# Key start, mask rows by DMA and a new instruction order in a fused sparse-attention and MLP kernel

## The chip, the cores and the metric

The kernel runs on one core of a Trainium2 chip. The metric is the device time of one execution in microseconds (us), as a median over several executions. Shorter is better.

The engines are named as the profile names them. PE is the matmul engine and PEld its weight loads, DVE is the vector engine, ACT the scalar engine, POOL the general one, and SP the engine that only issues DMA. A `q` after an engine's name is its instruction queue issuing DMA.

## The reference, cut to what matters

Block-sparse attention over 32 heads (4 batches of 8), 768 tokens, 64 dimensions, followed by a residual MLP that mixes tokens and then channels:

```python
scores = (q @ k.T) / 8                     # per head, 768 x 768
mask = window | first/last block | 3 random key blocks per query block    # 24 x 24 blocks of 32
attn = softmax(where(mask, scores, -1e9))
x = attn @ v                               # heads side by side: 4 x 768 x 512
u = x + lam * (w_tok @ (alpha1 * x + beta1))
out = u + lam * (relu((alpha2 * u + beta2) @ w_ch1) @ w_ch2)
```

## The kernel before

Heads are handled in 16 pairs, each pair in nine units. A unit is a score matmul group (L1020), one exp of 128 x 1024 on ACT (L1058), a multiplication and matmuls with the values (L1082). Token mixing (L1303) and channel mixing (L1450, L1530) of one batch run beside the attention of later ones.

Queries and keys come in as rows, so they are cast to bf16 and transposed on PE before the first score matmul can run. A query operand has 88 partitions: 64 dimensions and 24 **mask rows**, which add the random blocks' mask in the same matmul. The mask rows are the same for every head. They are computed once, into the first head of operand slot 0, and three more places (the second head of slot 0, and both heads of slot 1) need a copy of 24 x 768 bf16, which is 36 KB.

The start, cut:

```python
nc.sync.dma_start(q2f[:, 0, :], pair_ap(q, 0, 0)[:, 0, :])
nc.scalar.dma_start(k2f[:, 0, :], pair_ap(k, 0, 0)[:, 0, :])       # all keys of head 0 at once
# ...
keep_warm(6, 512); keep_warm(2, P)                                 # PE work without a use
# ... mask matmuls into bq_ps ...
first_cast(0, 0, nc.vector.tensor_copy)                            # queries of head 0
nc.scalar.activation(qx2[0][MB, 0, HS:S], bq_ps[1][0:NBLK, 0:HS], AF.Copy, bias=-BIG, scale=BIG)
nc.vector.tensor_scalar(out=qx2[0][MB, 0, 0:HS], ...)              # the two halves of the mask rows
nc.scalar.copy(out=relp[:, 0, 1, 0:P], in_=k2f[:, 0, 0:P])         # keys 0..127
nc.vector.tensor_copy(out=relp[:, 0, 1, P:HS], in_=k2f[:, 0, P:HS])
keep_warm(3, P)
for w, bk, o0, o1, cp in (
    (0, gbT[0], 0, 3, nc.vector.tensor_copy),                      # w = 0 queries, 1 keys
    (1, gbT[1], 0, 1, nc.scalar.copy),
    (1, gbT[2], 1, 3, nc.vector.tensor_copy),
):
    t = transposes(bk[:], lambda o: relp[:, 0, w, ts(o, P)], range(o0, o1))
    keep_warm(1 if w else 4, P)
    for r in range(2):
        cp(out=qkr[0][:, w, 0, o0:o1, r, :], in_=t[r * D : (r + 1) * D, o0:o1])
```

Everything after that goes through a list scheduler. Each operation has dependencies and a due time, shifted by an entry of a table `DUE` of about 1,400 tuned numbers. The scheduler simulates the engines at build time, and each engine then runs its instructions in that fixed order. The row copies were three scheduled DVE operations, and from unit 4 of the first pair (the first unit with blocks of its second head) a score matmul depends on the first of them:

```python
pl = Plan(..., dict(PE=5950, ACT=6100, DVE=6300, POOL=4000, SP=4000))   # when each engine is free, ns
# ...
for j in range(1, 4):
    def e_row(op, j=j):
        nc.vector.tensor_copy(out=qx2[j // 2][MB, j % 2, :], in_=qx2[0][MB, 0, :])
    ROWS.append(pl.dve(("row", j), dve(768, 4), (2, 6, 7)[j - 1], e_row))
# ...
if pi == 0:
    deps = [] if u < 4 else deps + ROWS[:1]
```

The softmax here doesn't subtract the row's maximum and nothing guards it: scores larger than these inputs give would overflow.

## Time and profile before

| | before |
|---|---|
| time | 305.74 us, median of 3 (305.52 to 305.75) |
| span of the profiled run | 304.0 us |
| start of the first channel-mixing matmul, called T | 54.51 us |
| span minus T | 249.49 us |
| first exp | 6.61 us |

The prediction below reads the engine table, slices, chain and timeline. How to read them: a timeline line gives the start and length of a run of equal instructions, then engine, line, operation, output and inputs. In brackets stands how long the engine was idle before it and what ended that wait. `x3` at the end means three instructions back to back. The chain of waits is followed backwards from the last instruction, so its shares say through which lines the end was set.

### The profile page before, as it was taken

How to read it: one execution, taken by the hardware profiler on the slowest of the kernel's cores; microseconds unless marked ns; L12 is line 12 of the kernel's file. 1: busy time of each engine (PE TensorE's matmuls, PEld its weight loads, DVE VectorE, ACT ScalarE, POOL GpSimd, SP SyncE). 2: the span in 40 equal slices, each digit the busy share in tenths (PEclk: the TensorE clock that was granted, in tenths of full speed). 3: DMA queues.
4: the chain of work that ended last, by engine and by line, in shares of the span. 5: the costliest groups of instructions: out<-in, count | busy, mean ns of one | idle time of the engine just before them, and what ended most of it. 6: DMA issues, size and time to landing. Idle time of an engine off the chain costs nothing.

```text
span 304.0 us, 7157 instructions
## 1 busy us (share of the span) xinstructions
PE 297.9 (98%) x2977; PEld 187.1 (62%) x2998; DVE 234.1 (77%) x441; ACT 177.5 (58%) x242; POOL 44.6 (15%) x71
## 2 busy tenths in 40 slices
PE   8999999999999999999999999999999999999996
PEld 4777888666656575566655565555664674565453
DVE  7779889988998995989878886668869681997212
ACT  4999999978778755775486756554557720000000
POOL 9457441150110120010000000000000000000000
PEclk9999999999999999999999999999999999999999
DMA  7999999999885969183252332050021004000111
GB/s 154 199 264 202 205 205 178 188 201 138 156 122 99 144 117 164 41 122 79 43 119 47 108 65 56 36 133 16 37 52 49 25 0 122 37 0 0 71 66 72
DMA packets 50672, 31.38 MB, mean 103 GB/s; under 512 B 27784, under 2 KB 47056, under 8 KB 50640
## 3 DMA queue, kind: packets, MB, share of 16 engines
q0 software_dynamic: 17520, 15.47, 32.8%
q1 hardware_dynamic: 32796, 15.06, 22.2%
q8 instruction: 23, 0.38, 0.5%
q10 hardware_dynamic: 324, 0.39, 0.4%
q14 instruction: 9, 0.07, 0.1%
HBM read 30.78 MB, written 6.29 MB: 122 GB/s over the span
## 4 chain that ended last, share of the span: by engine, by line
PE 91%; DVE 6%; ACT 1%; issue 1%; ACTq 0%
PE gb L1450 27%; PE gb L1530 27%; PE gb L1082 11%; PE gb L1303 9%; PE sps L1020 5%; PE sps L1039 4%; PE gb L1039 3%; PE gb L517 2%; PE gb L485 1%; DVE qk L579 1%; DVE a1p L1265 1%; DVE a1p L1254 1%; ACT eT L1058 0%; ACT qk L577 0%; DVE x_sb L1101 0%
## 5 line engine op out<-in xcount | busy, mean ns | idle before, releaser
L1058 ACT ACTIVATE eT<-sps 128x1024 f16<-128x1024 f32 x114 | 110.7, 1029 | 8.8 <-PE gb L1082 5.7
L1450 PE MATMUL gb<-uT,w1b 128*128 128x384 bf16 (+1 forms) x512 | 91.9, 326 | 0.0
L1530 PE MATMUL gb<-w2b,hts 128*128 128x512 bf16 (+2 forms) x379 | 87.2, 370 | 1.1
L1450 PEld LDWEIGHTS <-w1b 128*128 128x128 bf16 x512 | 48.5, 98 | 33.7 <-issue 1.9
L1063 DVE TENSOR_TENSOR eT<-eT,msk 128x1024 f16<-128x1024 f16 x90 | 59.7, 685 | 6.5 <-ACT eT L1058 6.4
L1530 PEld LDWEIGHTS <-hts 128*128 128x128 bf16 x400 | 36.6, 98 | 38.9 <-issue 1.9
L1058 ACT ACTIVATE eT<-gb 128x512 f16<-128x512 f32 x60 | 32.5, 594 | 33.7 <-PE gb L1039 31.8
L1497 DVE TENSOR_SCALAR hts<-gb,b1t 128x384 bf16<-128x384 f32 x73 | 44.9, 617 | 9.1 <-PE gb L1450 7.5
L1082 PEld LDWEIGHTS <-eT 128*128 128x128 f16 x1152 | 44.3, 97 | 10.8 <-issue 2.2
L1082 PE MATMUL gb<-vext,eT 128*128 128x65 f16 x1152 | 47.9, 193 | 0.1
L1489 ACT ACTIVATE hts<-gb,b1t 128x384 bf16<-128x384 f32 x55 | 31.5, 582 | 21.3 <-PE gb L1450 19.1
L1303 PE MATMUL gb<-a1p,wtokT 128*128 128x256 bf16 (+1 forms) x360 | 37.0, 251 | 0.0
L1552 DVE TENSOR_TENSOR ot<-x_sb,gb 128x512 f32<-128x512 f32 (+2 forms) x25 | 16.6, 665 | 25.9 <-PE gb L1530 25.9
L1303 PEld LDWEIGHTS <-wtokT 128*128 128x128 bf16 x360 | 29.5, 98 | 6.9 <-issue 1.9
L1020 PE MATMUL sps<-qk 88*128 88x512 bf16 (+1 forms) x144 | 31.3, 325 | 0.5 <-ACT eT L1058 0.3
L1327 DVE TENSOR_TENSOR x_sb<-x_sb,gb 128x512 f32<-128x512 f32 (+1 forms) x26 | 16.7, 642 | 2.9 <-PE gb L1303 2.5
L1101 DVE TENSOR_TENSOR x_sb<-gb,rcp 128x384 f32<-128x384 f32 x32 | 17.8, 558 | 1.1
L1039 PE MATMUL sps<-qk 64*128 64x256 bf16 x180 | 17.9, 305 | 0.0
L1098 DVE RECIPROCAL rcp<-gb 128x6 f32<-128x6 f32 x32 | 6.2, 193 | 13.2 <-PE gb L1082 13.2
L1039 PEld LDWEIGHTS <-qk 64*128 64x128 bf16 x240 | 9.3, 94 | 11.5 <-issue 7.1
L1341 DVE TENSOR_TENSOR ub<-x_sb,a_bc 128x512 bf16<-128x512 f32 (+1 forms) x26 | 16.1, 645 | 0.3
L648 POOL DMA_DIRECT2D q<-in_q_dram x15 | 10.7, 710 | 35.3 <-DMA qk<-q 29.7
(70 smaller groups left out, 173.4 us busy)
## 6 DMA issues: line engine op xcount, KB each, us to landing
out_dram<-ot SPq DMA_DIRECT2D x23, 256.0 KB, 2.0
v<-in_v_dram POOLq DMA_DIRECT2D x16, 192.0 KB, 7.9
k<-in_k_dram POOLq DMA_DIRECT2D x15, 192.0 KB, 6.5
q<-in_q_dram POOLq DMA_DIRECT2D x15, 192.0 KB, 7.2
w1b<-in_moe_w_ch_dram POOLq DMA_DIRECT2D x4, 512.0 KB, 11.4
w2b<-in_moe_w_ch_dram POOLq DMA_DIRECT2D x4, 512.0 KB, 16.9
qk<-qk SPq DMA_DIRECT2D x20, 96.0 KB, 3.0
wtk<-in_moe_w_tok_dram POOLq DMA_DIRECT2D x3, 384.0 KB, 8.6
```

The costliest lines, as they stand in the source:

```text
L1020: nc.tensor.matmul(spsT[sl(key[0])][:, o : o + w], kx2[i][0:KC, a, ts(jt, P)], qx2[i][0:KC, a, c : c + w], start=True, stop=True,)
L1039: nc.tensor.matmul(half(key, r)[:, o : o + w], kd[i][rows, h, g, :], qx2[i][rows, h, c : c + w], start=True, stop=True,)
L1058: nc.scalar.activation(out_, in_, AF.Exp, bias=EXPB, scale=SCALE)
L1063: nc.vector.tensor_tensor(out=e, in0=e, in1=msk[:, :, x : x + 512], op=ALU.mult)
L1082: nc.tensor.matmul(bk[:, t * VW : t * VW + D + 1], eTt[sl(("eT", i))][:, ts(col, P)], vx[:, a, jt, 0 : D + 1], start=(r == 0), stop=(r >= ...
L1101: nc.vector.tensor_tensor(out=x_sb[:, s0 : s0 + NT, h * D : (h + 1) * D], in0=o[:, :, 0:D], in1=rc[:].unsqueeze(2).broadcast_to([P, NT, D] ...
L1303: nc.tensor.matmul(bank(bk)[:, j * wp * P : (j + 1) * wp * P], wtokT[:, s, ts(m * g + j, P)], a1p[sl(ak)][:, s, 0:wp, :].rearrange("p w c ...
L1327: nc.vector.tensor_tensor(out=s, in0=s, in1=tp, op=ALU.add)
L1450: nc.tensor.matmul(bank(bk)[:, 0 : HS + w0], w1b[:, dk, ts(f, P)], rhs[dk], start=(dk == 0), stop=(dk == 3),)
L1489: nc.scalar.activation(htsT[hk][:, f, :], bank(bk)[:, w0 : HS + w0], AF.Relu, bias=b1t[:, f : f + 1], scale=1.0,)
L1497: nc.vector.tensor_scalar(out=htsT[hk][:, f, :], in0=bank(bk)[:, w0 : HS + w0], scalar1=b1t[:, f : f + 1], scalar2=0.0, op0=ALU.add, op1=A ...
L1530: nc.tensor.matmul(bank(ck)[:, cs], htsT[hk][:, nk, ts(mt, P)], w2h["t"][:, nk, cs], start=(nk == 0), stop=(nk == 15),)
```

## The change

Four things are done at once:

1. The first 128 key columns are loaded, cast and transposed ahead of the rest, to start the first score matmul earlier. The other 256 key columns are cast (`kr`), transposed (`kt`) and copied (`kc`) by scheduled operations.
2. The three row copies leave DVE and become DMA transfers issued on SP.
3. The transposes and copies are in another order and on other engines, and the warm-up matmuls between them are put behind them.
4. The due table is tuned anew for this start, which moves instructions of the whole kernel.

```diff
-    nc.scalar.dma_start(k2f[:, 0, :], pair_ap(k, 0, 0)[:, 0, :])
+    for c in (slice(0, P), slice(P, HS)):
+        nc.scalar.dma_start(k2f[:, 0, c], pair_ap(k, 0, 0)[:, 0, c])
 ...
+    nc.scalar.copy(out=relp[:, 0, 1, 0:P], in_=k2f[:, 0, 0:P])
     first_cast(0, 0, nc.vector.tensor_copy)
 ...
-    nc.scalar.copy(out=relp[:, 0, 1, 0:P], in_=k2f[:, 0, 0:P])
-    nc.vector.tensor_copy(out=relp[:, 0, 1, P:HS], in_=k2f[:, 0, P:HS])
-    keep_warm(3, P)
+    for j in range(1, 4):
+        nc.sync.dma_start(qx2[j // 2][MB, j % 2, :], qx2[0][MB, 0, :])
     for w, bk, o0, o1, cp in (
-        (0, gbT[0], 0, 3, nc.vector.tensor_copy),
         (1, gbT[1], 0, 1, nc.scalar.copy),
-        (1, gbT[2], 1, 3, nc.vector.tensor_copy),
+        (0, gbT[0], 0, 2, nc.vector.tensor_copy),
+        (0, gbT[2], 2, 3, nc.scalar.copy),
     ):
 ...
-        keep_warm(1 if w else 4, P)
 ...
-    keep_warm(3, P)
+    keep_warm(8, P)
-        dict(PE=5950, ACT=6100, DVE=6300, POOL=4000, SP=4000),
+        dict(PE=5600, ACT=5800, DVE=5600, POOL=4000, SP=4000),
 ...            (three DVE row operations out; kr, kt and two kc in)
+    ROWS = [landed(("row", j), 8200) for j in range(3)]
 ...
-            deps = [] if u < 4 else deps + ROWS[:1]
+            deps = [] if u < 1 else KREST[:1] if u == 1 else KREST if u < 4 else deps + ROWS[:1]
 ...            (the table DUE: all its numbers replaced)
```

`landed(..., 8200)` tells the scheduler to take the rows as being there at 8.2 us. The real wait is a semaphore.

## The prediction

> **What bounds the kernel now.** I read the page's engine table and slices first, to see which engine is full and when.
>
> ```profile
> PE 297.9 (98%) x2977; PEld 187.1 (62%) x2998; DVE 234.1 (77%) x441; ACT 177.5 (58%) x242; POOL 44.6 (15%) x71
> ...
> PE   8999999999999999999999999999999999999996
> ...
> DVE  7779889988998995989878886668869681997212
> ACT  4999999978778755775486756554557720000000
> ```
>
> PE (TensorE) looks full everywhere, but matmul ends are modelled, so I take PE's rate from the chain instead. ACT (ScalarE) is full only in slices 2 to 8, from about 8 to 61 us; DVE (VectorE) is at eight or nine tenths there. So there are two stages: a front of about 55 us, in which the exps on ACT release everything, and a long rest. The chain of work that ended last, asked for the stretch from 57 us to the end, then for 9 to 57 us, confirms it:
>
> ```profile
> by line: PE gb L1450 33.8%; PE gb L1530 33.4%; PE gb L1082 10.4%; PE gb L1303 9.8%; PE sps L1039 5.3%; PE gb L1039 3.9%; PE sps L1020 1.2%; issue 0.5%; DVE ot L1552 0.3%; PE gb L485 0.2%; PE gb L807 0.2%
> ...
> by line: PE sps L1020 26.2%; PE gb L1082 17.1%; PE gb L517 10.0%; PE gb L1303 8.7%; DVE qk L579 7.3%; issue 4.2%; DVE a1p L1265 3.8%; DVE a1p L1254 3.6%; ACT eT L1058 2.9%; ACT qk L577 2.8%; DVE x_sb L1101 2.4%; DVE wtokT L579 2.3%; DVE x_s
> ```
>
> After 57 us, all but about 1% of the chain is PE streaming: no start-up change can shorten that, only move it. Before 57 us the chain changes hands between PE, DVE and ACT. The hinge is the first channel-mixing matmul (L1450, 512 of them, 27% of the chain): from then on PE has a store of work. I call its start T. It is in the timeline, with the start-up that decides when exps begin:
>
> ```profile
> 4.49 0.48 ACT L530 ACTIVATE qk<-gb 24x384 bf16<-24x384 f32 x1 [0.95 <-PE gb L522]
> ...
> 4.99 0.30 ACT L541 CAST relp<-k2f 128x128 bf16<-128x128 f32 x1
> ...
> 5.61 0.55 ACT L553 COPY qk<-gb 64x128 bf16<-64x128 bf16 x2 [0.32 <-PE gb L517]
> ...
> 6.61 2.85 ACT L1058 ACTIVATE eT<-sps 128x1024 f16<-128x1024 f32 x3 [0.45 <-PE sps L1020]
> ...
> 6.67 0.77 DVE L997 COPY qk<-qk 24x768 bf16<-24x768 bf16 x2
> ...
> 8.80 0.51 PE L517 MATMUL gb<-identb,relp 128*128 128x128 bf16 x6 [0.52 <-DVE relp L512]
> ...
> 9.84 12.68 ACT L1058 ACTIVATE eT<-sps 128x1024 f16<-128x1024 f32 x13 [0.37 <-PE sps L1020]
> ...
> 53.36 0.36 DVE L579 COPY uT<-gb 128x384 bf16<-128x384 bf16 x1
> ...
> 54.51 0.82 PE L1450 MATMUL gb<-uT,w1b 128*128 128x385 bf16 x4
> ```
>
> The reader should see three things. The mask activation (L530) and the key cast stand in line on ACT before the first exp. The row copies L997 (0.77 us here, 0.35 more at 7.73) delay DVE's casts, PE then waits 0.52 us for those, and ACT 0.37 us for PE. And T is 54.5 us, just after DVE's last copy into uT.
>
> **What the Trainium skill says.** "VectorE: DVE Perf Modes", in its perf-mode tier table, lets a bf16 SBUF copy run four times faster than one element a cycle; 768 elements in 0.35 us (the single L997 copy) agrees, and shows that little DVE time is there to save. "DMA: Bandwidth & Descriptors", section on the anatomy of one DMA, gives a transfer about 2 us of fixed cost, most of it completion; small SBUF copies in this trace (qk<-qk, 96 KB) land in a median 3.0 us, so longer. "ScalarE: Activation LUTs", section on what ACT_TABLE_LOAD costs, measured about 1283 ns; here it is 1.28 us, from 2.26 us. "TensorE: Matmul & The Clock Gate", section on the back-to-back gap, has columns/2.4 + 2.5 ns warm, 216 ns for 512; four L1530 matmuls take 0.86 us of the chain, 215 ns each, in agreement.
>
> **The start, step by step.** Splitting the key load adds one issue on ACT's queue (0.36 us, as L452), so the table load moves from 2.26 to about 2.63 and ends at about 3.9. The cast of the first 128 key columns (0.30) then fits in ACT's former idle time before L530, ending near 4.2, against 5.29. It is off the path. The mask matmuls are not touched: L530's inputs come at 4.45, so it still ends at 4.97. The transposes of the first keys (PE) are done before that, where formerly they ended after 5.34. ACT now does two key copies (0.27 each, to 5.53) and, new, two copies of the third query slot (about 6.08). The first score matmul needs the first two query slots (two 64x256 DVE copies of 0.29 from 4.75) and the first keys, so starts near 5.4 instead of 5.98. But the first exp needs the third query slot as well: copies end at 6.08, two matmuls of 256 columns and their latency follow, exp at about 6.5. **The first exp gains only about 0.1 us**, although the first matmul gains 0.6. This is where I differ from the plan's own starting numbers, which have ACT free 0.3 us earlier.
>
> DVE loses the three row copies (0.77 + 0.35 = 1.1 us). The other key columns still need one 0.55 cast and two 0.29 copies, only later. The four casts and copies end by about 7.5, then the two casts of the second head (0.36 each) by 8.2, and the six transposes need no wait past the fourth exp's release. So **the 0.37 us hole before the fourth exp closes**. Exps after the first few are about 0.4 to 0.5 us earlier.
>
> **The rest of the front, from the new order.** I listed both kernels' instructions in order and multiplied counts by durations of the profile.
>
> ACT: exps cost 0.953 us each (7.61 for 8). Ahead of the 45th exp the kernel before has three 64x768 copies (0.75 each, as they pass in the timeline); the changed one has five such copies. That costs 1.5 us more than the start gained. The 43rd exp, which lets the 45th score block go, would end at 6.5 + 43 x 0.953 + 5 x 0.75 + about 1 us of leftover idle = 52.2.
>
> DVE: from the first query copy (5.22) to the last first-half uT copy (53.72 at its end) I count 45.2 us of work in 48.5. In the new order the same stretch holds 42.5 us, because the row copies left and two copies moved to ACT, with small shifts of other work. With the same 3.3 us of idle, starting at 4.75, it would end at 50.5.
>
> So ACT rather than DVE sets the new T. In the changed order the first L1450-type matmul comes directly after that 45th score block, so T is about 52.2 plus 0.45 for the three score matmuls, **52.7 (51.7 to 54) instead of 54.5: 1.8 us**.
>
> But the work left behind differs. Weighting each matmul with columns/2.4 (30.5 ns for the 65-column ones, from 24 in 0.73 us), PE has 44.6 us of useful work ahead of T before, and 43.4 after: 28 attention matmuls and some transposes are put off. That work comes back later: 1.2 x 1.04 = 1.25 us (1.04 from 245.7 us elapsed after T over 234.6 of such work). **Net: 1.8 - 1.25 = 0.55 us.**
>
> After T, the new order puts more work between exps: 16.8 us between the 45th and 54th score blocks instead of 10.6. There are few PE holes to fill: from T to the last score matmuls of this stage, at 65.6, PE had 11.1 us for 10.6 of work. I add 0.2 us. For the 200 us after that I add 0.3 us for a re-tuned order: by my column count its overhead there is about 10 us, mostly fixed per matmul, and in the chain only 1.2 us is "issue". Four warm-up matmuls fewer are worth nothing, they fill idle time.
>
> Sum: 0.55 + 0.2 + 0.3 = about 1.1 us. **Predicted: 304.6 us**, from 305.74.
>
> **Rivals.**
> 1. *The DMA for mask rows becomes the wait.* Three 24x768 copies are issued on SP after 5.0 and would land between 7.5 and 8.5 by the 3.0 us above. The fifth score block needs the first near 9.9. For it: the DMA line is at nine tenths through the front, and loads on POOL take 6.5 to 8 us. PE works in order, so a row landing at 11 would cost the exps 1 us: 305.5. Against: the same hardware queue's q2f copies, five times larger, land in 3.2 us. I give it 15%.
> 2. *ACT is the real bound and gets worse.* Five copies instead of three, and after the 45th exp a run of uT copy, three copies and two relus (about 3.8 us) with no exp between. If PE's attention matmuls starve there, T's gain is given back: 306 to 306.5. For it: ACT at nine tenths. Against: L1450 work is then ready, and it needs no exps.
> 3. *DVE was the real bound.* The chain passes through DVE from 17 to 33 us. If freeing 2.7 us of DVE moves T by the whole 3.2 us (53.7 to 50.5), the net gain is 2 to 2.5 us: 303.2. Against: ACT has no matching slack.
> 4. *The new order decides after T.* It may close holes that my counts don't see, or open some; PE lost about 4 us between 6 and 57 us by counts and a few more later. I give it 1 us either way.
>
> **Range and chances.** Rivals 1, 2 and 4 together give the upper end, 306.3; rivals 3 and 4 the lower, 302.7. Two per cent is 6.1 us. All the PE time lost in the front after 6 us is about 4 us, so a gain that large would need the later stage too: chance 0.03. A loss that large needs a stall that nothing here shows: 0.02. Within 2%: 0.95.
>
> **What would show it right or wrong.** Right: the first exp at about 6.5 while the first score matmul starts near 5.4; no ACT idle before the fourth exp; the first channel-mixing matmul at 51.7 to 54; rows landed before 9 us with no PE wait on them; PE's useful counts unchanged. Wrong: a PE wait on the DMA rows; the first exp near 6.3 (then ACT's copies are cheaper than I say); T after 54.5, or T near 50.5 (DVE was the bound); or T as predicted and the total not, which puts the cause in the order after T.

## More of the kernel before

One more view shows what the DMA engines did at the start. The rows of the windows view give: the stretch, its length, busy time of PE, PEld, DVE, ACT and POOL (with instruction counts), the granted PE clock, the busy share of the DMA engines, and GB/s.

```profile
6.00:9.00 3.00, 2.21 (x19) 1.31 (x20) 2.90 (x12) 2.55 (x4) 2.37 (x5) 1.00 1.19 152
9.00:20.00 11.00, 10.94 (x165) 8.67 (x163) 8.25 (x19) 10.34 (x12) 4.91 (x8) 1.00 1.17 224
```

From 6 us on the DMA share is at or above 1: the engines are full with bulk loads of the next heads and of the weights.

## The result, and the profile after

The changed kernel took **307.64 us** (median of 6, 307.09 to 307.82) against 305.75 us for the kernel before in the same rounds (median of 6, 305.52 to 306.29). The ratio is 1.0058, 95% interval 1.0045 to 1.0071. All ratios here are the mean time of one kernel's fast runs over that of the other's in the same rounds, so they are not quite the ratios of the medians. The time lies 1.3 us above the predicted range, and the sign is wrong.

The engine table and the PE, DVE and ACT slices of the changed kernel, with its chain over the whole span below them:

```profile
PE 300.1 (98%) x2994; PEld 187.4 (61%) x2994; DVE 230.4 (75%) x435; ACT 179.9 (59%) x247; POOL 45.0 (15%) x71
...
PE   8899999999999999999999999999999999999995
...
DVE  5398997998967789977789986758879871997122
ACT  4799999896668765789767755754566510000000
...
PE 95%; DMA 2%; ACT 1%; SPq 0%; issue 0%; DVE 0%; ACTq 0%
```

DVE lost 3.7 us of work (234.1 to 230.4), as intended, and its second slice (7.6 to 15.3 us) fell from 7 to 3 tenths. The chain has a new entry: 2% of it is now DMA. Before, there was none. The chain from 9 to 57 us says which transfer that is, first as shares and then as one piece with start and length:

```profile
by line: PE sps L1051 35.1%; PE gb L1113 22.7%; PE gb L1334 16.8%; DMA qk<-qk 11.3%; PE gb L521 11.0%; ACT eT L1089 4.6%; issue 1.7%; PE gb L1481 1.4%; PE gb L489 0.1%; ACTq L1089 0.0%
...
6.70 5.41 DMA qk<-qk
```

`qk<-qk` of 36 KB are the mask rows. The chain counts from the wrong issue here: 6.70 is the third copy's, and a partial update of that copy at 12.11 is the last one before PE goes on. The score matmul needs the first copy, and PE waits on that copy's semaphore. By the semaphore updates in the trace, the three copies were issued at 4.99, 5.92 and 6.70 and complete at 12.05, 12.88 and 13.23. So **the copy that PE waited for took 7.05 us from issue to landing**, and the 5.41 us and 11.3% above are too small. DVE, which had at least 19% of this stretch before (7.3, 3.8, 3.6, 2.4 and 2.3), is gone from it. The lines of the timeline that answer to those shown of before (L1051 scores, L1089 exps, L1481 first channel-mixing matmul):

```profile
4.39 0.89 PE L521 MATMUL gb<-identb,relp 128*128 128x128 bf16 x4
...
4.99 2.56 SPq L547 DMA_DIRECT2D qk<-qk  x3
...
5.93 1.06 PE L1051 MATMUL sps<-qk 88*128 88x512 bf16 x3
...
7.02 1.02 ACT L1089 ACTIVATE eT<-sps 128x1024 f16<-128x1024 f32 x1 [0.94 <-PE sps L1051]
...
8.71 2.85 ACT L1089 ACTIVATE eT<-sps 128x1024 f16<-128x1024 f32 x3 [0.66 <-PE sps L1051]
...
12.18 0.38 PE L1051 MATMUL sps<-qk 88*128 88x512 bf16 x1 [1.10 <-DMA qk<-qk]
...
12.59 1.02 ACT L1089 ACTIVATE eT<-sps 128x1024 f16<-128x1024 f32 x1 [1.03 <-PE sps L1051]
...
55.04 0.82 PE L1481 MATMUL gb<-uT,w1b 128*128 128x385 bf16 x4
```

Read it from above. The first exp starts at 7.02 us, not at 6.61. There is a hole of 0.66 us before the second exp. The fifth unit's score matmul (the first of the second head, so the first that needs a copied mask row) waits 1.10 us for the DMA, and ACT waits 1.03 us behind it. T is 55.04, not 54.51 and far from the predicted 52.7.

A second thing shows when each span is cut at T. The **span is T plus a remainder that belongs to the order of instructions**:

| kernel | order | span | T | span − T | median us | ratio (95%) |
|---|---|---|---|---|---|---|
| before | old | 304.0 | 54.51 | 249.49 | 305.75 | |
| changed | new | 305.8 | 55.04 | 250.76 | 307.64 | 1.0058 (1.0045 to 1.0071) |
| a_dve_rows | new | 304.1 | 53.68 | 250.42 | 305.88 | 1.0000 (0.9981 to 1.0019) |
| a_warm | new | 307.3 | 56.58 | 250.72 | 308.88 | 1.0096 (1.0076 to 1.0116) |
| a_dve_warm | new | 304.0 | 53.57 | 250.43 | 305.84 | 1.0015 (0.9973 to 1.0056) |
| b_dma_rows | old | 305.8 | 56.06 | 249.74 | 308.24 | 1.0076 (1.0043 to 1.0109) |
| a_dve_late | new | 304.6 | 54.18 | 250.42 | 306.31 | 1.0024 (1.0005 to 1.0042) |
| a_dve_late_warm | new | 305.1 | 54.69 | 250.41 | 306.00 | 1.0001 (0.9984 to 1.0017) |
| a_hold | new | 305.8 | 55.04 | 250.76 | 307.49 | 1.0058 (1.0043 to 1.0073) |
| a_old_start | new | 303.8 | 53.34 | 250.46 | 305.67 | 1.0006 (0.9986 to 1.0025) |
| a_best | new | 304.3 | 53.88 | 250.42 | 305.96 | 1.0001 (0.9986 to 1.0015) |
| b_late | old | 303.3 | 53.85 | 249.45 | 305.47 | 0.9996 (0.9983 to 1.0010) |
| after_2 (changed again) | new | 305.5 | 54.75 | 250.75 | 307.28, one run | |
| before_2 (before again) | old | 303.8 | 54.34 | 249.46 | 305.55, one run | |

Over all fourteen traces the remainder is 249.45 to 249.74 with the old order and 250.41 to 250.76 with the new one, while T varies by more than 3 us. So whatever a start-up edit is worth is read off T, and the new order costs about 1 us after T whatever the start is. The two last rows are single executions, whose state is unknown; they serve for their timelines only. Spans are rounded to 0.1 us, and the remainders with them. In the rounds of the experiments the kernel before had medians of 305.76 us (for all up to a_old_start) and 305.65 us (for a_best and b_late). All experiments gave correct results.

### The profile page after: what moved, and what is told of

It is laid out like the page before. It is cut to its first block, busy times and chain, and to the rows that moved or that the text cites. A ratio compares the mean times of both kernels' runs of the same rounds, so it can differ in the third digit from the quotient of the medians.

```text
span 305.8 us, 7180 instructions
## 1 busy us (share of the span) xinstructions
PE 300.1 (98%) x2994; PEld 187.4 (61%) x2994; DVE 230.4 (75%) x435; ACT 179.9 (59%) x247; POOL 45.0 (15%) x71
## 3 DMA queue, kind: packets, MB, share of 16 engines
q0 software_dynamic: 17520, 15.47, 32.4%
## 4 chain that ended last, share of the span: by engine, by line
PE 95%; DMA 2%; ACT 1%; SPq 0%; issue 0%; DVE 0%; ACTq 0%
PE gb L1481 27%; PE gb L1561 27%; PE gb L1113 12%; PE gb L1334 11%; PE sps L1051 7%; PE sps L1070 4%; PE gb L1070 3%; PE gb L521 2%; DMA qk<-qk 2%; PE gb L489 1%; ACT eT L1089 1%; SPq L547 0%; DVE ot L1583 0%; ACT qk L535 0%; PE gb L810 0%
## 5 line engine op out<-in xcount | busy, mean ns | idle before, releaser
L1089 ACT ACTIVATE eT<-sps 128x1024 f16<-128x1024 f32 x114 | 110.9, 1031 | 5.9 <-PE sps L1051 4.4
L1481 PE MATMUL gb<-uT,w1b 128*128 128x384 bf16 (+1 forms) x512 | 90.9, 326 | 0.0
L1561 PE MATMUL gb<-w2b,hts 128*128 128x512 bf16 (+2 forms) x400 | 89.3, 370 | 0.0
L1481 PEld LDWEIGHTS <-w1b 128*128 128x128 bf16 x512 | 48.7, 98 | 33.8 <-issue 1.9
L1089 ACT ACTIVATE eT<-gb 128x512 f16<-128x512 f32 x60 | 32.5, 594 | 40.0 <-PE gb L1070 39.9
L1528 DVE TENSOR_SCALAR hts<-gb,b1t 128x384 bf16<-128x384 f32 x72 | 44.1, 617 | 11.2 <-PE gb L1481 9.4
L1113 PEld LDWEIGHTS <-eT 128*128 128x128 f16 x1152 | 43.5, 97 | 10.7 <-issue 3.5
L1520 ACT ACTIVATE hts<-gb,b1t 128x384 bf16<-128x384 f32 x56 | 32.3, 583 | 20.8 <-PE gb L1481 13.2
L1051 PE MATMUL sps<-qk 88*128 88x512 bf16 (+1 forms) x144 | 32.6, 333 | 1.7 <-DMA qk<-qk 1.1
L1051 PEld LDWEIGHTS <-qk 88*128 88x128 bf16 x144 | 12.4, 99 | 7.5 <-issue 3.1
L651 POOL DMA_DIRECT2D q<-in_q_dram x15 | 10.6, 707 | 40.5 <-DMA qk<-q 35.0
```

What stands on the lines that cost most here:

```text
L1051: nc.tensor.matmul(spsT[sl(key[0])][:, o : o + w], kx2[i][0:KC, a, ts(jt, P)], qx2[i][0:KC, a, c : c + w], start=True, stop=True,)
L1089: nc.scalar.activation(out_, in_, AF.Exp, bias=EXPB, scale=SCALE)
L1113: nc.tensor.matmul(bk[:, t * VW : t * VW + D + 1], eTt[sl(("eT", i))][:, ts(col, P)], vx[:, a, jt, 0 : D + 1], start=(r == 0), stop=(r >= ...
L1481: nc.tensor.matmul(bank(bk)[:, 0 : HS + w0], w1b[:, dk, ts(f, P)], rhs[dk], start=(dk == 0), stop=(dk == 3),)
L1520: nc.scalar.activation(htsT[hk][:, f, :], bank(bk)[:, w0 : HS + w0], AF.Relu, bias=b1t[:, f : f + 1], scale=1.0,)
L1528: nc.vector.tensor_scalar(out=htsT[hk][:, f, :], in0=bank(bk)[:, w0 : HS + w0], scalar1=b1t[:, f : f + 1], scalar2=0.0, op0=ALU.add, op1=A ...
```

## The experiments

The theories after the first reading were these. **W**: the DMA row wait is what costs the time. **S**: the slow first exp comes from the removed warm-up matmuls, since PE ran its first weight loads at 0.15 us instead of 0.10. **O**: the new order costs about 1 us after T. They don't exclude each other, so each edit takes one away. `b_` kernels are built on the kernel before, `a_` kernels on the changed one.

### a_dve_rows: the row copies back on DVE, all else as changed

```diff
-    for j in range(1, 4):
-        nc.sync.dma_start(qx2[j // 2][MB, j % 2, :], qx2[0][MB, 0, :])
 ...
+    def e_kr(op):              # kr emits the key cast and the three copies behind it
+        nc.vector.tensor_copy(out=relp[:, 0, 1, P:HS], in_=k2f[:, 0, P:HS])
+        for j in range(1, 4):
+            nc.vector.tensor_copy(out=qx2[j // 2][MB, j % 2, :], in_=qx2[0][MB, 0, :])
```

> Changed kernel, but the three mask rows are copied by DVE right after its cast of the remaining first keys, into DVE idle time (1.31 us before the next copy in the changed kernel's trace); all other orders unchanged. Theory W (the DMA of the rows is what PE waits for: landing at 12.1 us, PE idle 1.1 us, ACT idle 1.03 us before the fifth exp): the wait goes, the fifth exp starts near 11.6 instead of 12.59, the time falls by about 1.0 us to 306.6. Rival S (PE runs at half rate until about 8.8 us and this delays the first exps): time stays within 0.3 us of 307.6. Rival O (the new order after the start costs the time): also stays.

Measured: 305.88 us, 1.76 us less than the changed kernel (307.64; I had expected 1.0), and equal to the kernel before (ratio 1.0000). T is 53.68, which is 1.1 to 1.4 us less than in the two traces of the changed kernel (54.75 and 55.04), and the remainder is 0.3 less. Its timeline:

```profile
6.24 1.11 DVE L996 COPY qk<-qk 24x768 bf16<-24x768 bf16 x3
...
8.62 10.30 ACT L1091 ACTIVATE eT<-sps 128x1024 f16<-128x1024 f32 x11 [1.17 <-PE sps L1053]
```

From the second exp on, eleven run without a hole: the hole of 1.03 us at the fifth exp has gone with the DMA. W holds. The three copies that the DMA was to spare cost 1.11 us of DVE. But they were put in a bad place: the copies of the rest of the keys stand behind them, so the second exp now waits 1.17 us instead of 0.66.

### b_dma_rows: the kernel before, with only the row copies by DMA

```diff
+    for j in range(1, 4):
+        nc.sync.dma_start(qx2[j // 2][MB, j % 2, :], qx2[0][MB, 0, :])
     nc.scalar.copy(out=relp[:, 0, 1, 0:P], in_=k2f[:, 0, 0:P])
 ...
         def e_row(op, j=j):
-            nc.vector.tensor_copy(out=qx2[j // 2][MB, j % 2, :], in_=qx2[0][MB, 0, :])
+            pass
```

> Kernel before, with its three row copies moved from DVE to DMA on SP at the place where the changed kernel issues them; order otherwise unchanged. Theory W: the first row lands near 12 us, PE waits for it before the fifth score block, the fifth exp (10.8 us in the kernel before) moves to about 12.5, and the time rises by 1.0 to 1.7 us to about 307. Rival (the wait is absorbed later because PE and not ACT sets the end): within 0.4 us of 305.75.

Measured: 308.24 us, 2.5 us more than the kernel before (305.76). The four executions fall into two groups, though, and their mean granted clocks tell them apart: 307.37 and 307.60 us at 1.000 and 0.999, 308.87 and 309.18 us at 0.992 and 0.994. The two at full clock are 1.6 to 1.8 us above the kernel before, which agrees with the 1.76 us of a_dve_rows from the other side. (The ratio in the table mixes both groups.) The profiled run is one of the two at full clock; its T rose by 1.55 to 56.06. So the DMA rows by themselves account for nearly all of what the whole change lost. Timeline:

```profile
12.12 0.38 PE L1022 MATMUL sps<-qk 88*128 88x512 bf16 x1 [1.95 <-DMA qk<-qk]
...
12.54 1.02 ACT L1060 ACTIVATE eT<-sps 128x1024 f16<-128x1024 f32 x1 [2.17 <-PE sps L1022]
```

In its chain the transfer is issued at 4.99 and takes 7.00 us, landing at 11.99. That is the first copy, issued at the same time as in the changed kernel, and it takes as long as there (7.05 us). The packet records of the changed kernel say what happens in between. There are 72 row packets of 1,536 bytes, 24 for each of the three copies. The first has been served at 9.6 us, the 24th at 10.6 and the last at 12.7. (A packet doesn't say to which copy it belongs, so the 24th need not be the end of the first copy.) Between 6.5 and 9.5 us only packets of the software queue, the bulk loads issued by POOL, were served: 634 of 768 bytes and 39 of at most 128. The DMA view of the changed kernel from 4 to 14 us, with packets, MB and share of the 16 engines:

```profile
q0 software_dynamic: 1520, 1.46, 95.0%
q1 hardware_dynamic: 282, 0.33, 10.6%
```

So the small copies seem to have stood behind loads that fill the engines. **The cost of the DMA would then be its place among queued loads, not its size.**

### a_hold: the bulk loads held until the rows are issued

To test that, a tiny POOL copy after the row DMAs makes POOL wait for the mask rows, so that its loads are issued at about 5.5 instead of 3.75 us.

```diff
     for j in range(1, 4):
         nc.sync.dma_start(qx2[j // 2][MB, j % 2, :], qx2[0][MB, 0, :])
+    held = wk.tile([P, 2], BF, name="held", tag="held")
+    nc.gpsimd.tensor_copy(out=held[MB, :], in_=qx2[0][MB, 0, 0 : HS + 1 : HS])
```

> Changed kernel, rows still by DMA, but a two-element copy on POOL that reads both halves of the finished mask row holds back the queued loads for the second pair and the token weights from 3.75 to about 5.1 us. Theory Q (the row packets wait behind the bulk loads issued before them: no packet of the first rows between 6.5 and 9.5 us in the changed kernel's trace): the first row lands before 10 us, PE no longer waits for it, and the time falls by 0.7 us or more, unless the later arrival of the second pair's keys and queries (1.3 us later) takes the wait's place after 12 us. Rival F (a small transfer inside SBUF has a fixed cost of 5 us here): it lands near 12 again and the time stays at 307.6 or above.

Measured: the first row packet is now served at 6.84 us and the 24th at 7.46, instead of 9.6 and 10.6. The first copy is complete at 7.90 instead of 12.05, that is 2.91 us after its issue instead of 7.05. No PE wait on the rows is left. Yet the time is 307.49 us, the same as the changed kernel's. Timeline:

```profile
8.61 10.47 ACT L1091 ACTIVATE eT<-sps 128x1024 f16<-128x1024 f32 x11 [0.56 <-PE sps L1053]
...
19.71 0.37 PE L521 MATMUL gb<-identb,wtk 128*128 128x128 bf16 x3 [1.02 <-DMA wtk<-in_moe_w_tok_dram]
...
20.61 9.62 ACT L1091 ACTIVATE eT<-sps 128x1024 f16<-128x1024 f32 x10 [1.53 <-PE sps L1053]
```

Eleven exps run through, and then the token-mixing weights are 1.02 us late, because their load was put off with the rest. So the bulk loads are shown to be what made the rows late. The gain was lost again because the wait moved to `wtk`: its second load is issued at 9.84 us instead of 7.64 and lands at 19.66 instead of 17.41, 9.8 us after its issue both times. Whether the DMA engines have anything to spare in this stage is not shown by this, since the edit put off all the later loads.

### a_warm and a_dve_warm: three warm-up matmuls ahead of the transposes

```diff
+    keep_warm(3, P)            # ahead of the transposes; a_dve_warm also has the edit of a_dve_rows
     for w, bk, o0, o1, cp in (
```

> Changed kernel, with the three warm-up matmuls of the kernel before put back ahead of the first transposes; rows still by DMA. Theory S (PE stays at half rate because it is less busy near 4.2 us): 128-column weight loads of the first score block fall from 0.15 to 0.10 us, the first exp starts near 6.5 instead of 7.02, but the row DMA still lands near 12 us, so under theory W the time changes by less than 0.3 us from 307.6. If S alone is right, it falls by 0.5 us or more.

> Both edits together: rows by DVE and the three warm-up matmuls. If W and S both hold and the order after the start is as good as I predicted: fifth exp near 10.6 us, time 305.0 to 305.7. If the new order itself costs time (rival O), the time stays at 306 or above although the fifth exp is at 10.8 us or earlier, as in the kernel before.

Measured: a_warm took 308.88 us, slower than the changed kernel by 1.2, and a_dve_warm 305.84 us, the same as a_dve_rows. In a_warm the first exp did come earlier (6.58), but the row still landed late, so that the hole before the fifth exp became 1.79 us, and two more follow. The windows view, first the changed kernel, then a_warm:

```profile
9.00:20.00 11.00, 9.59 (x148) 7.56 (x147) 6.48 (x14) 9.97 (x11) 5.17 (x9) 1.00 1.17 225
```

```profile
9.00:20.00 11.00, 8.97 (x108) 6.68 (x107) 4.96 (x11) 8.13 (x10) 5.04 (x8) 0.84 1.18 225
```

The granted PE clock in this stretch is 0.84 of full speed in a_warm, and PE gets through 108 instructions instead of 148. All four executions of a_warm had a mean clock of 0.993 or 0.994, like the two slower ones of b_dma_rows; all those of the changed kernel were at 0.999 or 1. The length of the wait on the DMA alone doesn't explain the clock: PE waited 1.65 us for it in a_warm, but 1.95 us in b_dma_rows, where the granted clock of the same stretch stayed at 1.00 in the profiled execution. The trace's clock records say more. In a_warm the clock is halved once, from 12.06 to 15.47 us. That is 3.41 us, and every complete stretch of one clock in the fourteen traces is a multiple of 3.41 us (3.41, 6.83, 293.55, 296.96 or 300.37). The windows view of a_warm, for the 3.41 us before the drop and for the drop itself:

```profile
8.65:12.06 3.41, 1.54 (x15) 0.78 (x11) 1.38 (x3) 2.41 (x3) 1.95 (x3) 1.00 1.19 217
12.06:15.47 3.41, 3.25 (x37) 2.49 (x38) 0.00 (x0) 1.92 (x2) 1.11 (x2) 0.50 1.22 250
```

PE was busy for 45% of the stretch before the drop. In b_dma_rows the boundary of such a stretch, at 11.39 us, cuts the wait in two, and the stretches on both sides are busy for 64% and 78%. The least busy one at full clock in the front of the other traces has 60%. So what seems to decide whether the clock drops, and another 1.5 us are lost, is whether the wait falls into a single stretch. This rests on one drop seen in a trace and was not tested.

Of my expectation for a_warm, the mechanism held: the first exp came earlier and was worth nothing in front of a transfer that lands at a fixed time. The time missed: I had expected no change beyond 0.3 us, and the lower clock made it 1.2 us longer.

### after_2: the changed kernel once more, one look

> The changed kernel once more, for its first 9 us alone: if the half rate of PE there (128-column weight loads at 0.15 us, first exp at 7.02) belongs to the kernel, it is seen again; if it varies between executions, the first exp may be near 6.5 here. The wait on the mask row must be seen either way.

This run decides theory S. The 128-column warm-up weight loads after the transposes, first in the changed kernel, then in the same kernel run again:

```profile
5.02 0.85 PEld L489 LDWEIGHTS <-const-bfloat16-1.0 128*128 128x128 bf16 x8 [0.28 <-issue]
```

```profile
5.02 0.50 PEld L489 LDWEIGHTS <-const-bfloat16-1.0 128*128 128x128 bf16 x8 [0.41 <-issue]
...
6.54 1.02 ACT L1089 ACTIVATE eT<-sps 128x1024 f16<-128x1024 f32 x1 [0.47 <-PE sps L1051]
...
11.89 0.38 PE L1051 MATMUL sps<-qk 88*128 88x512 bf16 x1 [1.59 <-DMA qk<-qk]
```

The same kernel took 0.85 us for these eight loads in one execution and 0.50 in another, and its first exp started at 7.02 or at 6.54. So PE's half rate at the start varies between executions of one kernel. The clock records agree: the first record of the full clock begins at 8.67 us in the changed kernel's trace and at 4.41 in after_2. S falls: without the warm-ups the slow start can stay away (here), and with them it can come (a_dve_late_warm, below). Whether they change how often it comes is not shown. (What the Trainium skill says on this stands at the end.) And at 6.54 the row wait grew from 1.10 to 1.59 us. Half a microsecond gained at the first exp was lost again at the fifth, apart from the 0.3 by which the row landed earlier.

### a_dve_late and a_dve_late_warm: the row copies later on DVE

To close the hole that a_dve_rows had before the second exp, the three copies follow the casts of the second head. a_dve_late_warm adds the three warm-up matmuls.

```diff
+    def e_fc(op, i):
+        first_cast(1, i, nc.vector.tensor_copy)
+        if i:
+            for j in range(1, 4):
+                nc.vector.tensor_copy(out=qx2[j // 2][MB, j % 2, :], in_=qx2[0][MB, 0, :])
```

> Changed kernel with the three row copies on DVE, but after its two casts for the second head instead of before the copies of the remaining first keys. In the run with early DVE rows they held those key copies back and the second exp began at 8.62 us after 1.17 us of idle time; here they fall into the 0.79 to 1.07 us in which DVE waits for the transposes. Theory W with an ACT-paced front: second exp near 7.5, fifth near 10.5, time 304.6 to 305.2, that is 0.7 to 1.2 us below the run with early rows. Rival P (what is gained before the first channel-mixing matmul is given back, because the new order leaves more work behind it): time stays within 0.3 us of 305.9.

> The same with the three warm-up matmuls put back before the first transposes. Theory: like the run with late rows, within 0.3 us; if PE in that run is still at half rate in the first 8 us, this one is up to 0.5 us faster.

Measured: 306.31 and 306.00 us. I missed: I had overlooked another DVE instruction between the two key copies. DVE's timeline of a_dve_late:

```profile
6.66 0.29 DVE L579 COPY qk<-gb 64x256 bf16<-64x256 bf16 x1 [0.60 <-PE gb L521]
7.46 0.26 DVE L758 CAST uT<-be2T 128x4 bf16<-128x4 f32 x1 [0.51 <-DMA be2T<-in_moe_beta_dram]
7.73 0.28 DVE L579 COPY qk<-gb 64x256 bf16<-64x256 bf16 x1
```

A cast of 4 columns waits 0.51 us for its own load, and the second key copy, for which PE and ACT wait, stands behind it in order. In a_dve_rows the row copies had filled that time. In a_dve_late_warm the profiled execution ran its weight loads at half rate in spite of the added warm-ups, which again speaks against S.

### a_old_start: the old start with the new order

```diff
-    for c in (slice(0, P), slice(P, HS)):
-        nc.scalar.dma_start(k2f[:, 0, c], pair_ap(k, 0, 0)[:, 0, c])
+    nc.scalar.dma_start(k2f[:, 0, :], pair_ap(k, 0, 0)[:, 0, :])
 ...    (casts, transposes, copies and warm-ups as in the kernel before)
-        lambda op: nc.vector.tensor_copy(out=relp[:, 0, 1, P:HS], in_=k2f[:, 0, P:HS]),
+        lambda op: [nc.vector.tensor_copy(out=qx2[j // 2][MB, j % 2, :], in_=qx2[0][MB, 0, :]) for j in range(1, 4)],
 ...    (kt and kc emit nothing)
```

> Start of the kernel before (all first keys cast, transposed and copied ahead, rows by DVE, one key load, all warm-up matmuls) with the new order of everything after. It measures the new order alone. If the order is neutral as my count said (1.8 us earlier at the first channel-mixing matmul, 1.25 us of work put off): 305.0 to 305.8. If the new order alone is worse: above 306.2. If it is what makes the run with early DVE rows as fast as the kernel before, about 305.9 too.

Measured: 305.67 us, ratio 1.0006: no difference from the kernel before, and within the 305.0 to 305.8 expected for a neutral order. In spans, T fell by 1.17 (54.51 to 53.34) and the remainder rose by about 1.0 (249.49 to 250.46). The new order does bring T forward, and gives back nearly all of it later. Its exps:

```profile
6.28 11.67 ACT L1087 ACTIVATE eT<-sps 128x1024 f16<-128x1024 f32 x12 [0.41 <-PE sps L1049]
```

Twelve exps without a hole from 6.28 us. **The old start feeds the exps better than the new one**, whose second exp waits for the rest of the keys in every variant. With this run the change splits up. The order alone is worth −0.1 us (305.67 against 305.76), the new start with the row copies on DVE +0.2 (305.88), and the copies by DMA +1.8 (307.64). They add up to the measured 1.9 us by the way they are formed, as steps from one run to the next. The first two lie within the noise (the interval of a_old_start reaches 0.14% below and 0.25% above the kernel before); only the third is clear of it.

### a_best and b_late: can either kernel be bettered?

Both leave the row copies on DVE, but one by one where DVE has time, and move the beta cast out of the way. a_best starts from the changed kernel: row 1 after the second head's casts, rows 2 and 3 with the beta cast after the first copy of the values. b_late starts from the kernel before:

```diff
-            lambda op, i=i: first_cast(1, i, nc.vector.tensor_copy),
+            lambda op, i=i: (first_cast(1, i, nc.vector.tensor_copy), None if i else row(1)),
 ...
+                    if pi == 0 and r == 1:       # after the second head's operand copies
+                        row(2)
+                        row(3)
+                        nc.vector.tensor_copy(out=be2u[:, :, 15], in_=be2T[:])
```

> Changed kernel with the first row on DVE after the casts of the second head, the other two after the copy of the first values, and the small beta copy moved out of the way of the second copy of the first keys (in the run with late rows, DVE stood 0.51 us for that beta load with the key copy behind it, and PE waited 1.0 us). If the front is exp-paced: second exp by 7.9 us, no hole over 0.5 us among the first five exps when PE is at full rate, first channel-mixing matmul at 53.0 to 53.4, span 303.4 to 303.9, time 305.1 to 305.6. Since the new order leaves 250.4 to 250.8 us after that matmul in all runs so far, against 249.5 to 249.7 in the order of before, it should not beat the kernel before by more than 0.6 us.

> Kernel before, with only the three row copies and the beta copy moved later on DVE (first row after the two casts, the rest after the copies for the second head). The 0.37 us hole before the fourth exp should close, and the first channel-mixing matmul move from 54.5 to about 54.1: time 305.3 to 305.6, the start's gain without any DMA and without a new order. If the hole is absorbed later: 305.75 unchanged.

Measured: a_best 305.96 us, ratio 1.0001, with a wide spread from 304.96 to 306.51. The expected gain was missed: a hole of 0.49 us is left before an exp, behind PE waiting for DVE's casts of the second head. b_late has 305.47 us, ratio 0.9996 (0.9983 to 1.0010). Its timeline shows the aim reached, with the exps running on from the first:

```profile
6.61 15.37 ACT L1065 ACTIVATE eT<-sps 128x1024 f16<-128x1024 f32 x16 [0.45 <-PE sps L1027]
```

The hole of 0.37 us of the kernel before has closed, and T fell from 54.51 to 53.85. The profiled span is 303.3 against 304.0 and 303.8 for the two traces of the kernel before. But the interval of the timing contains 1, so a gain is not shown. No version clearly beats the kernel before.

before_2, the kernel before once more, was run as the counterpart of after_2:

> The kernel before once more: in its first trace PE was at full rate from 4.4 us on. If this varies between executions, the first exp may lie anywhere from 6.2 to 7.1 us here; if it belongs to the kernel, it is at 6.6.

Its T of 54.34 and remainder of 249.46 lie beside the 54.51 and 249.49 of the first trace, so the differences of a microsecond in the table are not chance of a single trace.

## Why the prediction was wrong

**The step that failed** is the one that dismissed rival 1: the row copies "would land between 7.5 and 8.5 by the 3.0 us above". They landed at 12.05, 12.88 and 13.23, the first 7.05 us after its issue. I had even worked out the case "a row landing at 11 would cost the exps 1 us", but I gave it 15%. That ACT then waited 1.03 us is chance: the row came a microsecond later still, but the exps were late too, and in after_2, where they were not, ACT waited 1.51 us. In time I had put 0.9 us on this case (305.5 less 304.6). The mistake was in where the 3.0 us came from. It is the median of 20 transfers, nearly all of them later in the kernel, and my second witness, the q2f load with 3.2 us, was issued before the bulk loads filled the engines. Neither is a transfer issued at 5 to 7.5 us. The view that would have told me is the windows line shown above, with a DMA share of 1.19 from 6 to 9 us. I named it ("the DMA line is at nine tenths") and then took a duration from elsewhere. Alone, this step cost 1.76 us (a_dve_rows). b_dma_rows has the same size in the other order, and a_hold shows the mechanism.

The predicted T of 52.7 against 55.04 splits into these terms. The end of the 43rd exp, predicted at 52.2, was at 54.51, so all of the 2.3 us are found there (copies counted as they pass in the timeline):

| term | predicted | measured | difference |
|---|---|---|---|
| first exp | 6.5 | 7.02 | +0.5 |
| 43 exps | 41.0 | 40.95 | 0 |
| five copies on ACT | 3.75 | 3.55 | −0.2 |
| hole before the second exp | 0 | 0.66 | +0.66 |
| hole before the fifth exp (rows) | 0 | 1.03 | +1.03 |
| other idle time of ACT | 1.0 | 1.29 | +0.29 |

The other points of the prediction:

- **The first exp at about 6.5, no earlier than that.** Right where PE runs at full rate (6.54 in after_2, 6.42 in a_dve_rows), and 7.02 in the profiled execution at half rate. The first score matmul, predicted at 5.4, then started at 5.54 and 5.41.
- **The hole before the fourth exp closes.** It closed, and I overlooked that a new one opens before the second. The rest of the keys now passes a DVE cast, two transposes and two DVE copies after the first score block, with the beta cast between the copies. All variants of the new start have this hole, from about 0.2 us (a_best) to 1.2.
- **T is set by ACT and its copies.** The mechanism is supported: with the start of before, the new order's exps run through at first and T is 53.34 (a_old_start), lower by 1.17. I had 1.8. There ACT still had 1.7 us of idle time between the first exp and the 43rd, which ended at 52.81, where I put "about 1 us of leftover idle".
- **Work put off beyond T costs 1.25 us.** This size was about right: the remainder grew by about 1.0 in a_old_start. The traces agree with the count that I made before: after T, a_old_start has 820 attention matmuls of 65 columns where the kernel before has 792, and 12 transposes of queries and keys where that has 6 (counted by their start), while PE is idle there for 1.7 us in both. Putting this work off was not tested by itself.
- **0.2 and 0.3 us gained after T by the tuned order.** No trace shows either. These two were hopes, not readings; 0.5 of the predicted gain of 1.1 us rested on them.
- **The busy shares.** I read DVE "at eight or nine tenths" in slices 2 to 8; slices 2 and 3 show 7. No sum rests on it.
- **Within 2% with a chance of 0.95.** Right.
- **The four warm-up matmuls are worth nothing.** Right, as far as the timing of a_dve_warm against a_dve_rows can tell.

Rival 2 (ACT starves the later stage) and rival 3 (DVE was the bound) show nowhere: from T to 75 us PE was idle for less than 0.2 us in a_old_start as in the kernel before. DVE lost its place in the chain, and T did not fall to 50.5 in any run.

What stays open: why the hardware queue was served no row packets for some 3 us while the software queue was; why the remainder is another 0.3 us higher in the four traces of the new order with the rows by DMA (250.72 to 250.76 against 250.41 to 250.46), and likewise in b_dma_rows with the old order (249.74 against 249.45 to 249.49); whether the granted clock falls by the rule supposed at a_warm; and why some kernels scatter over more than a microsecond at full clock (one execution of a_dve_warm took 307.74, a_best 304.96 to 306.51).

## What to carry to other kernels

Three copies of 36 KB that together cost 1.1 us on a vector engine are not free when they are moved to DMA: their latency is that of the queue at that moment, so look at the DMA share in the stretch where they will be issued, and never take a duration from another stage. When a scheduler is told a landing time, measure it. And cut the span at a landmark: if the remainder after it follows the instruction order almost alone, every edit ahead of it can be judged by the landmark, and a start that comes sooner can be seen to be paid back later.

## What the Trainium skill lacked or had wrong

- "DMA: Bandwidth & Descriptors", section "Queues, rings and completion order", says that each engine "round-robins between the queue rows it has work for" by packets, and with the 2 us of fixed cost that the prediction quotes (from a section on DMAs issued by POOL, while these are issued on SP) a reader expects a small copy to land soon. Here the first 36 KB copy took 7.05 us (changed kernel) and 7.00 us (b_dma_rows) behind queued bulk loads, and 2.91 us with those held back (a_hold). In the changed kernel it was issued at 4.99 us, and no row packet was served before 9.6 us while the software queue moved on. When their descriptors were ready can't be seen in the trace, so this is a gap rather than a refutation: the page has no figure for a small copy in a full queue.
- "TensorE: Matmul & The Clock Gate", section "What's actually happening", calls the warm-up "run-variable". This agrees, with 0.85 or 0.50 us for the same eight weight loads in two executions of one kernel.
- No page says how a profile's table by stretches treats the time before the first clock record. It shows a granted clock of 1.00 from 6 to 9 us in the slow case too, although the first record begins only at 8.67 us and the weight loads before it run at half rate.
- No page has a figure for how far PE's load may fall within a stretch before its clock is lowered. Here the clock was halved for 3.41 us after a stretch that was 45% busy, and not after stretches of 60% and more (one drop seen).
